# Attention and mixture-of-experts on one core: the first expert's weight matrix in one load, the second batch's keys ahead of it

## Chip, core and metric

The kernel runs on one core of a Trainium2 chip. The metric is the device time of the run in microseconds. Five engines work side by side, each in its own fixed order of instructions: TensorE (PE, matrix products; PEld is its weight load), VectorE (DVE), ScalarE (ACT), GpSimd (POOL) and SyncE (SP). Sixteen DMA engines move data between the main memory (HBM) and the memory on the core; here GpSimd issues all loads and SyncE (at the end also ScalarE) the stores.

## The reference

Eight batches of 576 rows pass through an attention with pooled keys and values (eight heads, width 64), and the result, 4608 rows of 512, goes through a router that picks one of eight experts for each row.

```python
k_p = k.reshape(B, H, Sp, pool, D).mean(axis=3)      # 576 keys -> 72
v_p = v.reshape(B, H, Sp, pool, D).mean(axis=3)
scores = scale * np.matmul(q, k_p.transpose(0, 1, 3, 2))
attn = softmax(scores)                               # written out in the reference
x = np.matmul(attn, v_p)                             # as rows: (B*S, H*D)
...
logits = xn @ en.T / tau                             # cosine of row and expert
expert_idx = np.argmax(logits, axis=1)
h = np.maximum(x[mask] @ w1[e], 0.0)                 # w1[e]: 512 x 1024
out[mask] = gate_w[mask, None] * (h @ w2[e])         # w2[e]: 1024 x 512
```

## The kernel before

Each batch is one unit of work. All of its rows are sent through one guessed expert; the gate of a row whose expert is another one is zero, and a loop at the end adds what other experts owe. That loop isn't entered with these inputs.

**Stages of a batch b.** `attention(b)` loads keys (`load_k`), values (`load_v`) and queries (`load_q`), with a cast from float32 to float16 on the way. DVE adds the keys in groups and turns them (`k0`, `k1`, `kT`: L402 to L423), turns the queries in three units (`q0` to `q2`, L432), and adds the values (L445, L449). The mean of the values gives a guess of the expert (`mean`, `guess`, `guess_out`, L616 to L669). PE computes scores (L478), ACT the exponentials (L487), PE the weighted values (L498); DVE scales them (L508, L510) and turns them into `xt_all` (L533), three units again. Then the routing: squares on ACT (L539), products on PE (L553), and the gate on DVE and GpSimd (L570 to L609). `ffn(b)` makes h = relu(x w1) in eight parts (PE L782, ACT L790/L792), then y = h w2 in five row blocks (PE L801, L830; ACT L818/L839), and stores.

**Weights.** Four pairs of buffers (`held`) keep w1 and w2 of the last four batches' experts. Buffer 0 alone stores w1 in two halves of 512 columns, and `load_w1` fills it with two DMAs; the other three take w1 in one. The parts 0 to 3 of h wait for `lw1`, the parts 4 to 7 for `lw1b`, which is the same step except where b is 0 or 4. From batch 1 on a load is skipped when one of the four buffers already holds that expert; then DVE copies it (`copy_w`, L693) or nothing is to be done.

**Order of the loads.** Every load is a step of GpSimd, and `load()` chains each behind the one before, so their order is the order of the calls at L1036 and after. A step `reg` reads the guessed expert into a register of GpSimd and so holds the queue until the guess is there. Before the change the order at the start is: keys 0, a third of queries 0, values 0, the rest of queries 0, values 1; then `reg` 0, both halves of w1, keys 1, w2, queries 1, values 2; then `reg` 1, the next w1, keys 2, queries 2, w2, values 3.

**Order of all else.** `Plan` holds the steps with estimated durations, priorities and what they depend on. `order` simulates the engines and always takes the step that can start first, with the priority between those that can start at nearly the same time. `improve` then changes priorities at random for 400 rounds, with a fixed seed, and keeps what its model finds no slower. The instructions are emitted in that order; the engines don't reorder. Where the model sees the PE idle, above all in the first 28 us, `warm` (L371) puts dummy products in.

Of the kernel before, what the change touches and what calls it, by code (L numbers as in the profile page):

```python
# [12 lines left out]
FP16 = mybir.dt.float16  # L13
# [229 lines left out]
def kernel(  # L243
# [18 lines left out]
    F = moe_w1.shape[2]  # L262
# [12 lines left out]
    keep = ctx.enter_context(tc.tile_pool(name="keep", bufs=1))  # L275
# [15 lines left out]
    loads = {}  # L291
# [3 lines left out]
    def flat(a, b):  # L295
        return a[b].rearrange("h (i t) d -> (h i) (t d)", t=T)

    def grouped(a, b):
# [3 lines left out]
    NW = 4  # L302
# [1 line left out]
    code_c = keep.tile([1, NW, NW], FP32)  # L304
    weights = {}

    held = [(keep.tile([128, 2, 4, F // 2] if i == 0 else [128, 4, F], FP16, name=f"w1_{i}"),
             keep.tile([128, 4, 2, DM], FP16, name=f"w2_{i}")) for i in range(NW)]

    def w1_view(i):  # L310

        return held[i][0].rearrange("p h k f -> p k h f" if i == 0 else
                                    "p k (h f) -> p k h f", f=F // 2)

    def load_w1(i, e_val, half, cond=None):

        src = moe_w1[ds(e_val, 1)].squeeze(0).rearrange("(p w) f -> p w f", w=4)
        w1 = held[i][0]
        return nc.gpsimd.dma_start(  # L319
            out=w1[:, half] if i == 0 else w1, cond=cond,  # L320
            in_=src[:, :, ts(half, F // 2)] if i == 0 else src)

    def load_w2(w2, e_val, cond=None):
        return nc.gpsimd.dma_start(
            out=w2, cond=cond,
            in_=moe_w2[ds(e_val, 1)].squeeze(0).rearrange(
                "(w p r) d -> p w r d", p=128, r=2))
# [49 lines left out]
    def load(us, dma, emit, after=(), eng='POOL', hit=None):  # L377

        dma_last[0] = plan.step(eng, us, emit, after, dma=dma, seq=dma_last[0],
                                hit=hit)  # L380
        return dma_last[0]


    done = plan.named

    def attention(b, early=False):

        st = {}
# [290 lines left out]

        def weigh(i):  # L680

            w2 = held[b % NW][1]
            ld = (load_w1(b % NW, st['e'], i, st['miss']) if i < 2
                  else load_w2(w2, st['e'], st['miss']))
            st.setdefault('loads', ([], []))[i // 2].append(ld)

        def copy_w():
            code = reg(st['codes'][0:1, 0:1], ENG.DVE, NW)
# [67 lines left out]
    def ffn(plan, b, xt, w, get_gm, finish, last=False, early=0):  # L756
        st = {}
        w1v = w1_view(w).rearrange("p k h (w c r) -> p k h w r c", r=2, c=128)
        w2 = held[w][1]
        pri = 0.0 if b is None else float(b)  # L760

        def before(*names):
            return [] if b is None else [n if isinstance(n, tuple) else (n, b)
                                         for n in names]

        def h_part(w, u):


            if u == 0:
                st['ph', w] = psum(plan)  # L770
            ph = st['ph', w]
            for kk in range(4):
                x = xt()[:, kk]
                if w >= early:
                    to, of = ph[:, ds(u * 512, HALF)], x[:, ts(u, HALF)]
                elif u == 2:
                    to, of = ph[:, 512:256 + S], x[:, 256:S]
                else:
                    ms = (slice(0, 96), slice(96, 128))[u]
                    to, of = (a.rearrange("p (h m) -> p h m", h=2)[:, :, ms]  # L780
                              for a in (ph[:, 256:512], x[:, 0:256]))
                nc.tensor.matmul(out=to, lhsT=w1v[:, kk, w // 4, (w // 2) % 2, w % 2, :],  # L782
                                 rhs=of, start=(kk == 0), stop=(kk == 3))
# [62 lines left out]
        def chain(us, emit, after=(), tiles=0):  # L846
            o = plan.step('PE', us, emit, [*prev[0], *after], pri, tiles)
            prev[0] = [o]
            return o
# [4 lines left out]
        hs, relus = {}, []  # L854
        for w, u in order:
            end = 2 if w < early else 1
            xs = before('lw1' if w < 4 else 'lw1b', 'copy',
                        *(f'x{i}' for i in range(u + 1 if w < early else u + 2)))
            hs[w, u] = chain((0.33, 0.24, 0.54)[u] if w < early else 0.495, lambda w=w, u=u: h_part(w, u), xs,
                             tiles=int(u == 0))  # L860
            if u == end:
                if b is not None:
                    done['h', w, b] = hs[w, u]
                relus.append(plan.step('ACT', 0.57, lambda w=w: relu(w), [hs[w, u]], -10 + pri,
                                       frees=[(hs[w, 0], 0)]))
# [7 lines left out]
        for part in parts:  # L873
# [5 lines left out]
            c, half = part  # L879
# [34 lines left out]
    with tc.manual_schedule():  # L914
        def load_k(b, after=()):
            def emit():
                kk = loads['k', b] = inp.tile([128, T * D], FP16, name="kk")
                nc.gpsimd.dma_start(out=kk, in_=flat(k, b))
            done['lk', b] = load(0.6, 3.05, emit, [('k1', b - 2), *after])
# [22 lines left out]
        def load_expert(b, part=None):  # L942
            st = routes[b]
            if part in (None, 0):
                done['reg', b] = load(2.0 if b else 1.3, 0.0, st['chosen'],
                                      [('ix' if b == 0 else 'eb', b)])
            after = [('reg', b), ('y', b - NW)]
            us = (2.8, 2.8, 5.7) if b % NW == 0 else (5.6, 0.0, 5.7)
            for i, name in enumerate(('lw1', 'lw1b', 'lw2')):
                if us[i] == 0.0:  # L950
                    done[name, b] = done['lw1', b]
                elif part in (None, i // 2):
                    done[name, b] = load(0.65, us[i], lambda i=i: st['weigh'](i), after,
                                         hit=(b, 0.45, 0.02) if b > 1 else None)

        def first(eng, us, emit, after=(), dma=0.0):
# [46 lines left out]
        def pairs():  # L1003
# [11 lines left out]
            out=emb_h, in_=emb, func=AF.Square, accum_out=emb_n), [o_emb])  # L1015
# [4 lines left out]
            out=emb_n, in0=emb_n, in1=half_c[:E, 0:1], op=ALU.pow), [o_sq, o_ones])  # L1020
# [3 lines left out]
            out=ident_h, in0=irow, scalar1=icol, scalar2=None, op0=ALU.is_equal), [o_iota])  # L1024
# [8 lines left out]

        for b in range(B):
            attention(b, early=(b == 0))
        load_expert(0, 0)  # L1036
        load_k(1)
        load_expert(0, 1)
        load_q(1)
        load_v(2)  # L1040
        load_expert(1, 0)
        load_k(2)
        load_q(2)
# [57 lines left out]
    with tc.For_i(0, n_val[0], 1) as i:  # L1101
        f_val = nc.values_load(ext_i[0:1, ds(i, 1)], min_val=0, max_val=1)
        with tc.If(f_val > 0):
            b_val = nc.values_load(pair_b[0:1, ds(i, 1)], min_val=0, max_val=B - 1)
            e_val = nc.values_load(pair_e[0:1, ds(i, 1)], min_val=0, max_val=E - 1)
            for half in range(2):
                load_w1(0, e_val, half)
            load_w2(held[0][1], e_val)
            xt_c = inp.tile([128, T * D], FP16, name="qq").rearrange("p (w s) -> p w s", w=4)
            nc.vector.tensor_copy(  # L1110
                out=xt_c, in_=xt_all[:, ds(b_val, 1)].squeeze(1))
            gmx = rt.tile([128, NC], FP32, name="gm")
            nc.vector.tensor_copy(
                out=gmx,
                in_=oh_all[:, ds(b_val, 1), :, ds(e_val, 1)].rearrange("p b c e -> p (b c e)"))
            nc.vector.tensor_tensor(
                out=gmx, in0=gmx,
                in1=gate_all[:, ds(b_val, 1)].squeeze(1), op=ALU.mult)
            o_b = out[ds(b_val * S, S)]

            def add_rows(c, y_sb):
                o_sb = yp.tile([128, DM], FP32, name="y_sb")
                cols = DM if c < 4 else DM // 2
                for src, dst in out_rows(o_b, c, o_sb):
                    nc.sync.dma_start(out=dst, in_=src)
                nc.vector.tensor_tensor(out=y_sb[:, 0:cols], in0=y_sb[:, 0:cols],
                                        in1=o_sb[:, 0:cols], op=ALU.add)
                for dst, src in out_rows(o_b, c, y_sb):
                    nc.sync.dma_start(out=dst, in_=src)

            def finish(c, y_sb):
                if c != 3:
                    add_rows(c, y_sb)
                    return

                with tc.If(b_val < B - 1):
                    add_rows(c, y_sb)
                with tc.If(b_val > B - 2):
                    nc.vector.tensor_tensor(out=y_end, in0=y_end, in1=y_sb, op=ALU.add)

            px = Plan()
            ffn(px, None, lambda: xt_c, 0, lambda: gmx, finish)
            px.run()

# [37 lines left out]
```

The softmax here doesn't subtract the row's maximum and nothing guards it: scores larger than these inputs give would overflow.

## Time and profile before

The median of three runs is 213.88 us (213.76 to 214.06); the profiled execution has a span of 212.1 us.

| stretch, us | PE busy | DVE busy | ACT busy | granted PE clock | DMA, GB/s |
|---|---|---|---|---|---|
| 0 to 10 | 8.25 | 4.51 | 2.02 | 1.00 | 127 |
| 10 to 20 | 8.53 | 5.43 | 3.06 | 0.66 | 144 |
| 20 to 30 | 6.58 | 8.38 | 2.56 | 0.50 | 209 |
| 30 to 40 | 9.93 | 4.48 | 6.63 | 0.81 | 213 |
| 40 to 50 | 9.68 | 7.76 | 5.03 | 1.00 | 217 |
| 50 to 60 | 8.81 | 8.59 | 7.11 | 1.00 | 246 |

Each row is ten microseconds of the span, the busy columns are microseconds in it. PE's time includes the dummy products: 8.71 us in the first 11 us, 1.64 us from 20 to 30, 2.05 us from 50 to 60, 1.46 us from 100 to 102, none elsewhere. A line of the timeline reads: start, duration, engine, source line, operation, result and inputs, how many, and in brackets how long the engine was idle before and what ended it. L319 is the load of w1, L324 that of w2, L918 of keys, L932 of queries, L925 of values.

### The profile page before, as it was taken

Reading aid. Unit: us, or ns where it says so; the run is one execution under the profiler, and the core shown is the slowest. Engines: PE = TensorE matmul, PEld = TensorE weight load, DVE = VectorE, ACT = ScalarE, POOL = GpSimd, SP = SyncE. Lnnn points to the kernel's source line nnn. Section 1 sums busy time; section 2 is a strip of 40 time slices with the busy share of each in tenths; the row PEclk is TensorE's granted clock in tenths of the full one; section 3 lists DMA queues with packets and bytes.
Section 4 is the critical chain, followed back from the end, with each engine's and each line's share of the span. In section 5 each row is a group of like instructions: output and inputs, shape, how many; then the busy total and the mean of one; then the engine's idle time right before and its main releaser. Section 6 shows DMA issues by size and latency. Waiting matters only on the chain.

```text
span 212.1 us, 7648 instructions
## 1 busy us (share of the span) xinstructions
PE 192.6 (91%) x3270; PEld 119.9 (57%) x3271; DVE 145.8 (69%) x415; ACT 123.9 (58%) x195; POOL 38.9 (18%) x69
## 2 busy tenths in 40 slices
PE   6979849999898899999899899999899999999970
PEld 2455527646476467556575467646664677467520
DVE  2756793669798956975997689879778989106020
ACT  3024226585576568668583597657786689556420
POOL 7308041302220044003203302400200020002000
PEclk9975558999999999999999999999999999999995
DMA  4996999999999149999994899999970510051052
GB/s 77 186 188 104 209 214 207 213 210 247 254 220 162 52 78 204 245 223 252 245 215 43 180 246 255 215 217 246 256 174 3 159 66 6 0 166 61 2 173 57
DMA packets 18182, 34.63 MB, mean 163 GB/s; under 512 B 2008, under 2 KB 9048, under 8 KB 17632
## 3 DMA queue, kind: packets, MB, share of 16 engines
q0 software_dynamic: 12096, 24.65, 62.9%
q1 hardware_dynamic: 5680, 9.00, 13.6%
q8 instruction: 26, 0.43, 0.8%
q10 hardware_dynamic: 368, 0.46, 0.7%
q14 instruction: 12, 0.10, 0.2%
HBM read 61.88 MB, written 9.44 MB: 336 GB/s over the span
## 4 chain that ended last, share of the span: by engine, by line
PE 54%; DVE 7%; ACT 4%; issue 2%; ACTq 0%; DVEq 0%
PE pa L782 21%; PE pa L801 20%; PE pa L498 4%; PE pa L478 3%; PE pa L830 3%; PE pa L553 2%; DVE x_sb L510 2%; DVE vv L445 2%; DVE xt_all L533 1%; ACT at L487 1%; ACT sq L539 1%; DVE rc L508 0%; PE pa L616 0%; ACT y_sb L818 0%; DVE k L414 0%
## 5 line engine op out<-in xcount | busy, mean ns | idle before, releaser
L782 PE MATMUL pa<-xt_all,w 128*128 128x288 f16 (+3 forms) x576 | 71.7, 279 | 4.6 <-DVE xt_all L533 4.5
L782 PEld LDWEIGHTS <-w 128*128 128x128 f16 x576 | 50.2, 100 | 20.3 <-issue 7.1
L801 PE MATMUL pa<-w,hT 128*128 128x512 f16 x256 | 59.5, 380 | 0.4 <-ACT y_sb L818 0.3
L487 ACT ACTIVATE at<-pa 72x768 f16<-72x768 f32 x48 | 36.8, 802 | 10.4 <-PE pa L478 10.3
L792 ACT ACTIVATE hT<-pa 128x576 f16<-128x576 f32 x48 | 31.2, 650 | 13.1 <-PE pa L782 12.7
L801 PEld LDWEIGHTS <-hT 128*128 128x128 f16 x256 | 23.7, 98 | 26.8 <-issue 1.1
L818 ACT ACTIVATE y_sb<-pa,gm 128x512 f32<-128x512 f32 x29 | 19.1, 685 | 25.0 <-PE pa L801 23.6
L533 DVE STREAM_TRANSPOSE xt_all<-x_sb 128x256 f16<-128x256 f16 (+2 forms) x48 | 24.8, 555 | 0.7
L432 DVE STREAM_TRANSPOSE qT<-qq 128x768 f16<-128x768 f16 x24 | 22.5, 958 | 3.0 <-DMA qq<-in_q_dram 2.7
L510 DVE TENSOR_TENSOR x_sb<-pa,rc 128x768 f16<-128x768 f32 x24 | 23.0, 958 | 0.8
L539 ACT ACTIVATE sq<-xt_all 128x1024 bf16<-128x1024 f16 (+1 forms) x16 | 18.6, 1160 | 8.3 <-DVE xt_all L533 8.2
L570 POOL TENSOR_TENSOR rn<-lgT,half_c 128x5 f32<-128x5 f32 x8 | 9.5, 1186 | 62.9 <-DVE lgT L575 62.9
L478 PE MATMUL pa<-qT,kT 32*72 32x192 f16 (+2 forms) x512 | 17.1, 259 | 0.7 <-DVE x_sb L510 0.5
L319 POOL DMA_DIRECT2D w<-in_moe_w_dram x10 | 4.1, 414 | 70.2 <-DMA w<-in_moe_w_dram 23.9
L498 PE MATMUL pa<-vpx,at 72*32 72x65 f16 x1152 | 14.9, 201 | 1.9 <-ACT at L487 1.8
L498 PEld LDWEIGHTS <-at 72*32 72x32 f16 x1152 | 11.8, 100 | 8.2 <-ACT at L487 4.8
L371 PE MATMUL pa<-ones_m 128*128 128x512 f16 x45 | 13.9, 458 | 1.7 <-DVE half_c L1008 1.7
L508 DVE RECIPROCAL rc<-pa 128x12 f32<-128x12 f32 x24 | 5.3, 222 | 14.4 <-PE pa L498 14.0
L478 PEld LDWEIGHTS <-kT 32*72 32x72 f16 x512 | 10.9, 116 | 7.3 <-issue 2.5
L575 DVE STREAM_TRANSPOSE lgT<-pa 128x160 f32<-128x160 f32 x8 | 2.8, 345 | 17.7 <-PE pa L553 17.7
L925 POOL DMA_DIRECT2D vv<-in_v_dram x16 | 10.5, 670 | 16.0 <-DMA w<-in_moe_w_dram 6.7
L445 DVE TENSOR_TENSOR vv<-vv 72x2048 f16<-72x2048 f16 (+1 forms) x14 | 13.1, 938 | 0.3
(99 smaller groups left out, 160.4 us busy)
## 6 DMA issues: line engine op xcount, KB each, us to landing
w<-in_moe_w_dram POOLq DMA_DIRECT2D x14, 1024.0 KB, 15.9
out_dram<-y_sb SPq DMA_DIRECT2D x30, 256.0 KB, 7.3
kk<-in_k_dram POOLq DMA_DIRECT2D x8, 576.0 KB, 15.2
vv<-in_v_dram POOLq DMA_DIRECT2D x8, 512.0 KB, 24.4
qq<-in_q_dram POOLq DMA_DIRECT2D x7, 576.0 KB, 15.7
w<-in_moe_w_dram POOLq DMA_DIRECT2D x4, 512.0 KB, 5.7
out_dram<-y_sb SPq DMA_DIRECT2D x15, 64.0 KB, 8.4
vv<-in_v_dram POOLq DMA_DIRECT2D x8, 64.0 KB, 10.5
```

Source lines behind the costliest of these rows:

```text
L432: nc.vector.transpose(out=qT.rearrange("p w r (t i) -> p t w r i", i=16), in_=qq.rearrange("p t (w r i) -> p t w r i", w=2, r=2))
L445: nc.vector.tensor_tensor(out=vv[:, :, 0:n], in0=vv[:, :, 0:n], in1=vv[:, :, n:2 * n], op=ALU.add)
L478: nc.tensor.matmul(out=pS[a // 2][0:G, ds(a % 2 * 512 + r * SU + c0, n)].rearrange(dst, **dd), lhsT=kT[ts(a, 32), w, r, :], rhs=qT[ts(a, 3 ...
L487: nc.scalar.activation(out=at.rearrange("g a r c -> g a (r c)"), func=AF.Exp, scale=escale, in_=st['pS', u][p][0:G].rearrange("g (a c) -> ...
L498: nc.tensor.matmul(out=px[ts(a, 32), c0:c0 + D + 1], lhsT=st['at', u, a // 2][:, a % 2, r, ts(j, 32)], rhs=st['vpx'][:, 2 * a + r, 0:D + 1 ...
L510: nc.vector.tensor_tensor(out=x_sb, in0=pxv[:, :, :, 0:D], in1=rc.unsqueeze(3).to_broadcast([128, 2, 6, D]), op=ALU.mult)
L533: nc.vector.transpose(out=to, in_=of)
L539: nc.scalar.activation(out=st['sq'][:, :, cs], in_=xt_all[:, b, :, cs], func=AF.Square)
L782: nc.tensor.matmul(out=to, lhsT=w1v[:, kk, w // 4, (w // 2) % 2, w % 2, :], rhs=of, start=(kk == 0), stop=(kk == 3))
L792: nc.scalar.activation(out=hT.rearrange("p (r c) -> p r c", c=HALF), func=AF.Relu, in_=st['ph', w].rearrange("p (r c) -> p r c", c=512)[:, ...
L801: nc.tensor.matmul(out=py, lhsT=st['hT', w // 4][:, (w // 2) % 2, w % 2, ts(c, 128)], rhs=w2[:, w // 2, w % 2, :], start=(w == 0), stop=(w ...
L818: nc.scalar.activation(out=y_sb, in_=py, func=AF.Copy, scale=g)
```

## The change

Buffer 0 gets the same layout as the others, so w1 is one load in all four, and `lw1b` disappears: all parts of h wait for `lw1`. In the first and fifth batches there is one load step fewer. The keys of batch 1 move ahead of the first expert's `reg` and weights, so that they don't have to wait until the guess is known. The planner's estimates are adapted (1.8 for the first `reg`, 5.5 for each weight load).

```diff
-    held = [(keep.tile([128, 2, 4, F // 2] if i == 0 else [128, 4, F], FP16, name=f"w1_{i}"),
+    held = [(keep.tile([128, 4, F], FP16, name=f"w1_{i}"),
...
-    def load_w1(i, e_val, half, cond=None):
-
-        src = moe_w1[ds(e_val, 1)].squeeze(0).rearrange("(p w) f -> p w f", w=4)
-        w1 = held[i][0]
+    def load_w1(i, e_val, cond=None):
         return nc.gpsimd.dma_start(
-            out=w1[:, half] if i == 0 else w1, cond=cond,
-            in_=src[:, :, ts(half, F // 2)] if i == 0 else src)
+            out=held[i][0], cond=cond,
+            in_=moe_w1[ds(e_val, 1)].squeeze(0).rearrange("(p w) f -> p w f", w=4))
...
-            xs = before('lw1' if w < 4 else 'lw1b', 'copy',
+            xs = before('lw1', 'copy',
...
-                done['reg', b] = load(2.0 if b else 1.3, 0.0, st['chosen'],
+                done['reg', b] = load(2.0 if b else 1.8, 0.0, st['chosen'],
                                       [('ix' if b == 0 else 'eb', b)])
             after = [('reg', b), ('y', b - NW)]
-            us = (2.8, 2.8, 5.7) if b % NW == 0 else (5.6, 0.0, 5.7)
-            for i, name in enumerate(('lw1', 'lw1b', 'lw2')):
-                if us[i] == 0.0:
-                    done[name, b] = done['lw1', b]
-                elif part in (None, i // 2):
-                    done[name, b] = load(0.65, us[i], lambda i=i: st['weigh'](i), after,
+            for i, name in enumerate(('lw1', 'lw2')):
+                if part in (None, i):
+                    done[name, b] = load(0.65, 5.5, lambda i=i: st['weigh'](i), after,
                                          hit=(b, 0.45, 0.02) if b > 1 else None)
...
+        load_k(1)
         load_expert(0, 0)
-        load_k(1)
         load_expert(0, 1)
```

More of the change, by code (lines that the diff above doesn't have):

```diff
@@ L305 @@
     weights = {}
-    held = [(keep.tile([128, 2, 4, F // 2] if i == 0 else [128, 4, F], FP16, name=f"w1_{i}"),
+    held = [(keep.tile([128, 4, F], FP16, name=f"w1_{i}"),
              keep.tile([128, 4, 2, DM], FP16, name=f"w2_{i}")) for i in range(NW)]
     def w1_view(i):
-        return held[i][0].rearrange("p h k f -> p k h f" if i == 0 else
-                                    "p k (h f) -> p k h f", f=F // 2)
-    def load_w1(i, e_val, half, cond=None):
-        src = moe_w1[ds(e_val, 1)].squeeze(0).rearrange("(p w) f -> p w f", w=4)
-        w1 = held[i][0]
+        return held[i][0].rearrange("p k (h f) -> p k h f", f=F // 2)
+    def load_w1(i, e_val, cond=None):
         return nc.gpsimd.dma_start(
-            out=w1[:, half] if i == 0 else w1, cond=cond,
-            in_=src[:, :, ts(half, F // 2)] if i == 0 else src)
+            out=held[i][0], cond=cond,
+            in_=moe_w1[ds(e_val, 1)].squeeze(0).rearrange("(p w) f -> p w f", w=4))
     def load_w2(w2, e_val, cond=None):
@@ L680, in weigh @@
         def weigh(i):
[L682 to L685, printed above, removed]
+            ld = (load_w2(held[b % NW][1], st['e'], st['miss']) if i
+                  else load_w1(b % NW, st['e'], st['miss']))
+            st.setdefault('loads', ([], []))[i].append(ld)
         def copy_w():
@@ L1105 @@
             e_val = nc.values_load(pair_e[0:1, ds(i, 1)], min_val=0, max_val=E - 1)
-            for half in range(2):
-                load_w1(0, e_val, half)
+            load_w1(0, e_val)
             load_w2(held[0][1], e_val)
```

## The prediction

> **What bounds the kernel now.** I read the busy shares first, then the 40 slices, because an average hides a start that differs from the rest.
>
> ```profile
> PE 192.6 (91%) x3270; PEld 119.9 (57%) x3271; DVE 145.8 (69%) x415; ACT 123.9 (58%) x195; POOL 38.9 (18%) x69
> PEclk9975558999999999999999999999999999999995
> DMA  4996999999999149999994899999970510051052
> ```
>
> TensorE (PE) is busy for 91% of the span, so the end is set by its work plus the holes in it. The granted clock is half in slices 4 to 6 (about 16 to 32 us). Then the windows of ten microseconds: from 30 to 200 us the PE is idle for 6.1 us in all, and the first three windows hold 1.75, 1.47 and 3.42 us. A part of its busy time is filler, the dummy products of `warm` (L371): 3.5 us of it after 50 us. Next the DMA view of 15 to 32 us, 40 columns of 0.425 us, where the change acts:
>
> ```profile
> DMA  8700000599999999999999999989999999999999
> ```
>
> The rings stand empty from about 15.9 to 18.0 us, a hole of 2.1 us, and are full afterwards. The timeline names what ends the hole:
>
> ```profile
> 7.03 0.23 POOL L1005 IOTA pair_e<- 1x64 int32 x1
> 16.65 1.53 POOL L319 DMA_DIRECT2D w<-in_moe_w_dram  x2 [9.38 <-issue]
> 18.17 0.55 POOL L918 DMA_DIRECT2D kk<-in_k_dram  x1
> ```
>
> GpSimd sits for 9.38 us in `reg` until the first expert is known, and the second batch's keys stand behind it in the queue although they need nothing. Last, the timeline of PE and DVE, to see whether the first expert's weights are what the PE waits for:
>
> ```profile
> 25.55 1.44 PE L782 MATMUL pa<-xt_all,w 128*128 128x192 f16 x8
> 27.16 1.01 DVE L533 STREAM_TRANSPOSE xt_all<-x_sb 128x512 f16<-128x512 f16 x2
> 29.82 0.37 PE L782 MATMUL pa<-xt_all,w 128*128 128x64 f16 x4 [2.83 <-DVE xt_all L533]
> 36.63 0.35 DVE L575 STREAM_TRANSPOSE lgT<-pa 128x160 f32<-128x160 f32 x1 [3.47 <-PE pa L553]
> 40.76 2.69 DVE L432 STREAM_TRANSPOSE qT<-qq 128x768 f16<-128x768 f16 x3
> 56.82 1.74 PE L782 MATMUL pa<-xt_all,w 128*128 128x320 f16 x12 [0.91 <-DVE xt_all L533]
> ```
>
> No. The first eight products start at 25.55 with no wait. Dense work starts at 29.82, after 2.83 us on DVE's last transposes of x. By the semaphore updates of the trace the halves of the first w1 landed at 22.3 and 25.9. The second stall is the one that interests me: in the window of 51 to 58.5 us the PE is idle for 7.5 - 6.31 = 1.2 us and fills 2.05 us, because x of batch 1 isn't ready. Its chain begins with the transposes of q at 40.76.
>
> **What the Trainium skill says.** "DMA: Bandwidth & Descriptors", section "Queues, rings and completion order": on each DMA engine descriptors are consumed in ring order. So the keys, issued first, go ahead of w1 and can delay it. The trace agrees: the last updates come in the order of issue, first w1 22.3 and 25.9, keys 28.0, w2 33.4, q 37.0, v 39.7, next w1 44.4. The same page, section "Bandwidth", has 6.15 us for 1 MB; the trace has about 5 us for a whole w1 here, which I use. "TensorE: Matmul & The Clock Gate", Part 1, says that the full clock returns after about 3.4 us of sustained work. The trace agrees: work is dense from 29.82 and the clock share is 0.50 up to 33, 0.64 in the next microsecond, 1.00 after it. Nothing in the change brings that forward.
>
> **The change, part by part.**
>
> *Keys of batch 1 ahead of `reg`.* GpSimd is free at 7.3, and a second kk buffer is fresh, so they are issued there at 0.55 us, in time that is idle now. They queue behind the values of batch 1, whose landing is at 16.3 to 16.8. A transfer of 576 KB takes 2.75 us, the step between the earliest updates of keys and of the second half of w1 (23.81 to 26.56). They land at about 16.3 + 2.8 = 19 instead of 28.0. The hole is filled.
>
> *First w1 whole.* One issue of 0.6 us replaces two (1.53 us): 0.9 us less on GpSimd, hidden by the full rings. The page's packet times are by size in the trace: 1024 bytes take 98 ns, 8192 bytes 625 ns. Two halves are 64 small packets an engine, 6.3 us of packet time; whole it is 8 large ones, 5.0 us. The observed steps are smaller (about 5.6 for both halves), so I take a saving of 0.6 us, between 0 and 1.3. The start: the keys' data end near 18, the issue at 16.65 lets data flow at about 18.0 as now. So w1 is whole at about 18.0 + 5.0 + 1 = 24.0 to 25.0. The early products, which now need only the half that landed at 22.3, start at 25.55 today: they lose nothing at 25, and up to about 1 us at a late end of 26.5, which the wait until 29.82 absorbs.
>
> *Everything queued behind.* w2, q, v of the start come earlier by keys plus saving, 2.75 + 0.6 = 3.4 us: w2 at 30.0 (used at 39.84, no gain by itself), q at 33.6, v at 36.3. The next w1 waits for the second expert (issue 28.23), yet the rings still hold work then, so that group too comes some 3 us earlier.
>
> *What that is worth.* DVE idles 3.47 us ahead of 36.63, and now q isn't there (37.0). With q at 33.6, its three transposes, 2.69 us, fit into that hole, and with them the scores and exponentials of batch 1 can start up to 6 us earlier. The stall at 51 to 58 is 3.2 us. That is the upper bound of this step.
>
> *What it may cost.* Adding, halving and turning the keys takes 0.71 + 0.46 + 0.78 + 0.77 = 2.7 us of DVE, today at 30.3 to 33.2, where nobody waits for them. With the keys there at 19, the planner will set them between 20 and 30 us, where DVE is busy for 8.38 of 10. 1.6 us fit, 1.1 us don't, and they push the last transposes of x and with them the dense start. A price of 0 to 1.1 us; I take 0.8.
>
> *The order.* `Plan.improve` draws its random changes over the list of steps. Two steps (`lw1b` of batches 0 and 4) vanish and one is moved, so the draws differ and all engines' orders are found anew. Idle time and filler from 30 to 200 us are 6.1 + 3.5 = 9.6 us, what an order can win at the utmost. I take +-1.5 us for a new draw.
>
> *The rest.* For batch 4 one skipped load fewer, 94.29 to 94.80, 0.5 us on an idle GpSimd: nothing. The weight copies (L693, 1.22 us each) and PE's weight reads have the same sizes: nothing. The loop over other experts isn't entered.
>
> Sum of the likeliest case: of the 3.2 us about two thirds is won at 51 to 58 (-2.1), since the later stages are held by DVE, busy 8 to 9 of 10 there, and give some back; dense start +0.8. -1.3 us: 213.9 - 1.3 = 212.6.
>
> **The rivals.**
>
> *Hidden anyway (no change).* The page says that PE waits for no DMA but for v at the start (1.5 us). If the planner keeps the transposes of q behind the gate of batch 0, as at 40.76, earlier landings only lengthen the time that data lie there. Against it: DVE takes what can start first, and q would be there before the routing result. Time: 213.9.
>
> *Slower.* DVE becomes the bound of the start: the key work goes ahead of x, +1.1 us, and the new order moves the stalls elsewhere without winning the one at 51 us. The whole w1 also takes away the slack that early products have with a half. For it: DVE's 8.38 of 10 and its fixed order, in which a step that waits holds up all behind it, as with the second guess now (1.02 us idle ahead of 25.73, with x waiting). Time: 213.9 + 1.1 = 215.0, with an unlucky order up to 216.
>
> *Faster at full.* All of the 3.2 us and no price at the start: 210.7.
>
> **How the numbers follow.** Likeliest -1.3: 40%; full gain 15%; no change 13%; slower 32%. The faster cases give 0.55, within 0.2% (0.43 us) 0.13, slower 0.32. The range goes from 210.6 (full gain) to 215.5 (slower with part of the unlucky order).
>
> **What would show it.** Keys issued near 7 us and no hole in the DMA row at 16 to 18; the first w1 landed by 25 us; the group of w2, q, v some 3 us earlier; q of batch 1 turned ahead of the first routing result (L575); fewer fillers and no wait at 51 to 58. The slower case shows as a dense start of L782 past 30.5, with kk work (L402, L408, L414) between the x steps. I am wrong if dense work starts at the same time, q is turned early, and the PE's idle time later grows all the same: then the order found anew decides, not the loads.

## The result, and the profile after

The changed kernel takes 210.76 us (median of four runs, 210.49 to 211.59) beside 213.97 us for the kernel before: ratio 0.9846, interval 0.9802 to 0.9891. Run once more beside the experiments it gave 210.03 us and a ratio of 0.9868 (0.9811 to 0.9925). So the change makes the kernel about 1.3 to 1.5% faster.

Repeats of one kernel lie in steps here: of 98 runs of the kernel before, those with a mean clock share of 0.948 or more took 211.5 to 212.8 us (one took 213.84), those at 0.941 to 0.945 took 213.1 to 214.3 us, and the 14 at 0.936 or 0.937, which the ratios leave out as slow, 215.0 to 215.8 us. One profile against another is therefore good to about 2 us, and the ratios with their intervals decide.

The page after, the same rows as before:

```profile
PE 192.9 (92%) x3281; PEld 118.9 (57%) x3282; DVE 145.4 (70%) x415; ACT 124.0 (59%) x195; POOL 38.1 (18%) x67
PEclk9985589999999999999999999999999999999996
DMA  4999999899999249999998999999940600061052
```

PE's busy time is the same to 0.3 us while the span went from 212.1 to 208.8. That sum hides two things: the dummies rose from 45 to 56 (13.9 to 17.5 us), and the half clock ends 6.5 us sooner (27.2 in place of 33.7 us; the sixth slice has an 8). The DMA view of 15 to 32 us, 40 columns of 0.425 us:

```profile
DMA  9999999984997999799599999999999999999999
```

The hole of 2.1 us has gone. The timeline shows the first loads of GpSimd, then PE and DVE where the prediction looked:

```profile
7.20 0.59 POOL L913 DMA_DIRECT2D kk<-in_k_dram  x1
16.38 0.54 POOL L315 DMA_DIRECT2D w<-in_moe_w_dram  x1 [8.58 <-issue]
34.43 0.61 POOL L315 DMA_DIRECT2D w<-in_moe_w_dram  x1
...
22.72 7.14 PE L367 MATMUL pa<-ones_m 128*128 128x512 f16 x22
29.92 0.49 PE L777 MATMUL pa<-xt_all,w 128*128 128x192 f16 x4
...
24.84 1.04 DVE L529 STREAM_TRANSPOSE xt_all<-x_sb 128x512 f16<-128x512 f16 x2
31.30 0.17 DVE L641 MAX8 mx<-pa 128x8 f32<-128x8 f32 x1 [3.24 <-PE pa L634]
32.83 0.35 DVE L571 STREAM_TRANSPOSE lgT<-pa 128x160 f32<-128x160 f32 x1
37.95 2.69 DVE L428 STREAM_TRANSPOSE qT<-qq 128x768 f16<-128x768 f16 x3
```

Three readings. The keys go out at 7.20. DVE has all of x of batch 0 turned by 25.9 (24.84 + 1.04), against 30.4 before, and the second guess (MAX8) comes after it, at 31.30 instead of 25.73. And yet h starts at 29.92, because 22 dummies keep the PE from 22.72 on. The queries of batch 1 are still turned after the routing result, at 37.95.

Progress is best read from the first product of each batch's last row block (L830 before, L825 after), where the PE ends a batch's y:

| batch | 0 | 1 | 2 | 3 | 4 | 5 | 6 | 7 |
|---|---|---|---|---|---|---|---|---|
| before, us | 49.90 | 77.03 | 97.39 | 122.22 | 144.48 | 166.52 | 187.21 | 198.98 |
| after, us | 49.71 | 74.12 | 96.50 | 118.31 | 140.51 | 162.91 | 183.63 | 195.40 |
| gained so far | 0.2 | 2.9 | 0.9 | 3.9 | 4.0 | 3.6 | 3.6 | 3.6 |

The gain comes in two places, batch 1 (of which 2 us are given back in batch 2) and batch 3; from batch 4 on both kernels run at the same pace. Batch 3 is a stall that the prediction hadn't looked at. The timeline of the kernel before there:

```profile
97.39 1.06 PE L830 MATMUL pa<-w,hT 128*64 128x256 f16 x16
98.39 0.83 PE L782 MATMUL pa<-xt_all,w 128*128 128x192 f16 x8
99.16 0.74 PE L498 MATMUL pa<-vpx,at 72*32 72x65 f16 x48
99.83 0.41 PE L782 MATMUL pa<-xt_all,w 128*128 128x64 f16 x8
100.08 1.46 PE L371 MATMUL pa<-ones_m 128*128 128x512 f16 x6
102.31 0.97 PE L782 MATMUL pa<-xt_all,w 128*128 128x320 f16 x6 [0.78 <-DVE xt_all L533]
```

The last weighted values of batch 3 (L498) come after y of batch 2 is done; h then waits for DVE to scale and turn them, 2.2 us of dummies and idling (100.08 to 102.31). After the change they come before, and h runs on. The order already differs further ahead: DVE turns the first queries of batch 3 at 81.81 in place of 85.75, and PE has its first scores at 83.05 in place of 87.80.

```profile
94.65 0.56 PE L494 MATMUL pa<-vpx,at 72*32 72x65 f16 x48
95.55 1.02 PE L796 MATMUL pa<-w,hT 128*128 128x512 f16 x4 [0.34 <-ACT y_sb L813]
96.50 1.06 PE L825 MATMUL pa<-w,hT 128*64 128x256 f16 x16
97.50 2.65 PE L777 MATMUL pa<-xt_all,w 128*128 128x192 f16 x28
```

### The profile page after: what moved, and what is told of

Read it like the earlier page. It is cut to its first block, busy times and chain, and to the rows that moved or that the text cites. A ratio compares the mean times of both kernels' runs of the same rounds, so it can differ in the third digit from the quotient of the medians.

```text
span 208.8 us, 7667 instructions
## 1 busy us (share of the span) xinstructions
PE 192.9 (92%) x3281; PEld 118.9 (57%) x3282; DVE 145.4 (70%) x415; ACT 124.0 (59%) x195; POOL 38.1 (18%) x67
## 4 chain that ended last, share of the span: by engine, by line
PE 53%; ACT 5%; DVE 5%; issue 2%; ACTq 0%; DVEq 0%
PE pa L796 21%; PE pa L777 19%; PE pa L474 4%; PE pa L494 3%; PE pa L825 3%; PE pa L549 2%; ACT sq L535 2%; ACT y_sb L813 1%; ACT at L483 1%; DVE qT L428 1%; DVE vv L441 1%; DVE x_sb L506 0%; ACT y_sb L834 0%; DVE k L410 0%; DVE kT L419 0%
## 5 line engine op out<-in xcount | busy, mean ns | idle before, releaser
L777 PE MATMUL pa<-xt_all,w 128*128 128x288 f16 (+3 forms) x576 | 69.5, 273 | 0.8 <-DVE xt_all L529 0.8
L777 PEld LDWEIGHTS <-w 128*128 128x128 f16 x576 | 48.6, 98 | 15.0 <-issue 2.8
L483 ACT ACTIVATE at<-pa 72x768 f16<-72x768 f32 x48 | 36.8, 802 | 9.7 <-PE pa L474 9.5
L787 ACT ACTIVATE hT<-pa 128x576 f16<-128x576 f32 x48 | 31.2, 650 | 13.6 <-PE pa L777 13.5
L428 DVE STREAM_TRANSPOSE qT<-qq 128x768 f16<-128x768 f16 x24 | 22.6, 959 | 3.2 <-DMA qq<-in_q_dram 2.8
L367 PE MATMUL pa<-ones_m 128*128 128x512 f16 x56 | 17.5, 480 | 1.7 <-DVE half_c L1000 1.7
L494 PE MATMUL pa<-vpx,at 72*32 72x65 f16 x1152 | 14.3, 201 | 2.2 <-ACT at L483 2.1
L315 POOL DMA_DIRECT2D w<-in_moe_w_dram x8 | 3.1, 391 | 58.5 <-DMA w<-in_moe_w_dram 19.1
L367 PEld LDWEIGHTS <-ones_m 128*128 128x128 f16 x56 | 6.3, 119 | 10.7 <-issue 6.3
```

Of the source, the lines that this page charges most:

```text
L367: nc.tensor.matmul(out=pa[:, 0:512], lhsT=ones_m[:, 0:128], rhs=ones_m[:, 0:512], start=True, stop=True)
L428: nc.vector.transpose(out=qT.rearrange("p w r (t i) -> p t w r i", i=16), in_=qq.rearrange("p t (w r i) -> p t w r i", w=2, r=2))
L483: nc.scalar.activation(out=at.rearrange("g a r c -> g a (r c)"), func=AF.Exp, scale=escale, in_=st['pS', u][p][0:G].rearrange("g (a c) -> ...
L494: nc.tensor.matmul(out=px[ts(a, 32), c0:c0 + D + 1], lhsT=st['at', u, a // 2][:, a % 2, r, ts(j, 32)], rhs=st['vpx'][:, 2 * a + r, 0:D + 1 ...
L787: nc.scalar.activation(out=hT.rearrange("p (r c) -> p r c", c=HALF), func=AF.Relu, in_=st['ph', w].rearrange("p (r c) -> p r c", c=512)[:, ...
```

## The experiments

Two things changed at once, the loads and, through the planner with its new list of steps and its adapted estimates, the order of every engine. The first theories: **1**, the earlier loads themselves are the gain, as predicted; **2**, the dummies are, by bringing the PE's clock up sooner; **3**, the new order is. "Replanned" means that the planner made a new order for the variant; the others keep an order and alter one thing in it.

**Loads alone, order kept.** The step `lk` of batch 1 moves in the finished order to just ahead of the step `reg` of batch 0:

```diff
-        for o, slots, idle, spare in self.order(bias)[1]:
+        out = self.order(bias)[1]
+        at = {o['i']: n for n, (o, _, _, _) in enumerate(out)}
+        keys, reg = (at[self.named[x]['i']] for x in (('lk', 1), ('reg', 0))) if ('lk', 1) in self.named else (0, 0)
+        if keys > reg:
+            out.insert(reg, out.pop(keys))
+        for o, slots, idle, spare in out:
```

> The kernel before, with one thing altered: the keys of batch 1 are issued ahead of the first reg, after the planner has made its order; both halves of w1 and the order of every other engine stay as they were. Theory 1 (earlier loads are the gain, as the prediction had it): q and v land some 3 us earlier, time falls by 1 us or more, 212.9 or less. Theory 2 (the PE clock is the gain: dummy products ahead of the first expert bring it to full 6.5 us sooner): no gain, 213.7 to 214.1, clock at half until about 33.7 us. Theory 3 (only the new order found by the planner counts): no gain either, 213.7 to 214.1.

213.55 us, ratio 0.9989 (0.9955 to 1.0024): no gain that can be told. The loads did come sooner; by the trace's semaphore updates the keys landed at 20.0 in place of 28.0, w2 at 31.4 in place of 33.4, q at 34.6 in place of 37.0. DVE made no use of it:

```profile
36.78 0.35 DVE L580 STREAM_TRANSPOSE lgT<-pa 128x160 f32<-128x160 f32 x1 [2.97 <-PE pa L558]
40.87 2.69 DVE L437 STREAM_TRANSPOSE qT<-qq 128x768 f16<-128x768 f16 x3
```

It idles for 2.97 us ahead of the routing result with q there from 34.6, since q's transposes stand behind that result in its order. Theory 1 as it stood (a gain of 1 us or more, some 0.5%) is refuted.

**The clock alone.** Dummies in the PE's hole of the kernel before, at the second unit of h of batch 0:

```diff
+            if b == 0 and w == 0 and u == 1:
+                for _ in range(14):
+                    nc.tensor.matmul(out=ph[:, 0:256], lhsT=ones_m[:, 0:128], rhs=ones_m[:, 0:256],
+                                     start=True, stop=True)
```

> The kernel before, with 14 dummy products of 256 columns put into the PE's hole of 2.83 us ahead of the 29.8 us mark (their results are never read); loads and order as before. Theory 2 (clock): full clock at about 27 to 29 us in place of 33.7; the 3.9 us of dense work that ran at half clock takes 1.9 us less: 212.0. Theories 1 (loads) and 3 (order): no gain, 213.9, or 0.2 more where the dummies overrun the hole.

212.81 us, ratio 0.9979 (0.9955 to 1.0003). In the profile the full clock came during the microsecond 26 to 27, in place of 33 to 34, so the clock was moved as meant, but it is worth between nothing and 0.45%, short of the 0.9% that theory 2 gave it and of the change's 1.3 to 1.5%. (In its profile the last row blocks of batches 0 and 7 start at 47.62 and 197.37, 2.3 and 1.6 us ahead of the kernel before. That is more than the ratio shows, and about what two profiles of one kernel can differ by.)

**The dummies taken out of the changed kernel:**

```diff
+        if 18 < t < 30:
+            n = 0
```

> The changed kernel without the 22 dummy products ahead of the first expert's h; loads and order as in the changed kernel. They kept the PE from 22.7 to 29.9 us, while w1 had landed at 25.0 and x of all rows at 25.9. Theory 2 in its plain form (the clock they bring is the gain): the gain of 3.2 us is lost in good part, 212.5 to 213.5. Theory 2 with its price (h starts at 25 in place of 29.9, runs at half clock for some 3.5 us and then at full): 4.9 us sooner, 1.8 us lost to the clock, a net gain on the changed kernel of up to 3 us, 208 to 209.5. Theory 1: the dummies only cost, 206 to 208.

210.69 us, ratio 0.9877 (0.9825 to 0.9929), not told apart from 0.9846 and 0.9868 with them. None of the three expectations fits. What shows is a swap: the PE now starts h 4.3 us sooner, at the landing of w1, and at half clock.

```profile
25.59 0.82 PE L779 MATMUL pa<-xt_all,w 128*128 128x192 f16 x4 [3.57 <-DMA w<-in_moe_w_dram]
```

```profile
PEclk9995559999999999999999999999999999999997
```

Two things are to be seen: w1 whole is now really waited for (3.57 us), where the half had landed in time; and starting sooner at half clock and starting later at full clock come out even as far as the intervals tell. So the 22 dummies aren't the gain, and no loss from them shows.

**Each half of the change, replanned.** Keys early, w1 in halves:

```diff
+        load_k(1)
         load_expert(0, 0)
-        load_k(1)
         load_expert(0, 1)
```

> Half of the change: keys of batch 1 ahead of the first reg, in the planner's list of steps so that a new order is found, with w1 in two halves as before. The planner now sets 13 dummies ahead of h in place of 3. Theory 1 (loads): most of the gain, 211 to 212. Theory 2 (clock): part of it, since 13 dummies at half clock last 5.6 us, full clock at about 27 to 29: 211 to 212.5. Theory 3 (order): anything from 212 to 215.5.

210.11 us, ratio 0.9894 (0.9835 to 0.9953): most or all of the gain, and a time below all three expected ranges. And w1 whole with the keys in their old place (the changed kernel with `load_k(1)` put back behind `load_expert(0, 0)`; the adapted estimates stay):

> The other half of the change: w1 whole in all four buffers, keys of batch 1 still behind the first w1, new order by the planner. It has 22 dummies ahead of h as the changed kernel, and DVE turns all of x of batch 0 ahead of the second guess as there, but keeps the dummies of the later stall in batch 3. Theory A (the early keys let the planner find the better order): no gain, 213.3 to 214.5. Theory B (any new draw, or the DVE order at the start alone): 210.5 to 212.

214.94 us, ratio 1.0100 (1.0056 to 1.0144): slower, by more than either theory had it. The stall of batch 3 is there as in the kernel before, though x of batch 0 is done by 26.2, ahead of the second guess at 30.9:

```profile
98.35 0.56 PE L494 MATMUL pa<-vpx,at 72*32 72x65 f16 x48
98.84 0.41 PE L777 MATMUL pa<-xt_all,w 128*128 128x64 f16 x8
99.09 1.46 PE L367 MATMUL pa<-ones_m 128*128 128x512 f16 x6
101.33 1.74 PE L777 MATMUL pa<-xt_all,w 128*128 128x320 f16 x12 [0.79 <-DVE xt_all L529]
```

So with these draws the keys carry the gain, and w1 whole (with the adapted estimates, which weren't tried apart) costs when it comes alone. Together with the first experiment this means: the keys help only through the order that the planner makes when it knows of them.

**The order without the early landing.** The changed kernel's order, keys issued behind the first w1 when the program is written out:

```diff
+            keys = next(x for x in out if x[0] is self.named['lk', 1])
+            out.remove(keys)
+            at = next(n for n, x in enumerate(out) if x[0] is self.named['lw1', 0])
+            out.insert(at + 1, keys)
```

> The changed kernel with its planned order on every engine, but the keys of batch 1 issued behind the first w1 when the program is written out. Keys land near 27 to 28 us in place of 19 to 20, w1 some 2 us sooner, w2 and q up to 2 us later because of the hole. DVE takes the keys at 26.8 and the PE has dummies until 29.9, so at most 1 us of waiting on DVE. If the order is the gain and not the landing: 210.5 to 211.5. If the early landing itself is needed: 212.5 or more.

211.33 us, ratio 0.9893 (0.9859 to 0.9928). The order brings most of the gain with the keys landing at 27.8. Between this ratio and those of the changed kernel lie 0.25 to 0.5%, which the intervals don't tell apart from nothing; if the early landing adds anything, it is of that size. My working in the expectation was off for w1: it landed at 25.1, not sooner than in the changed kernel.

**One stretch of the order in the kernel before.** The second guess behind the last turn of x on DVE, with the GpSimd steps that hang on it:

```diff
+            a = next(n for n, x in enumerate(out) if x[0] is self.named['eb', 1])
+            z = next(n for n, x in enumerate(out) if x[0] is self.named['x1', 0])
+            late = [x for x in out[a:z] if x[0] is self.named['eb', 1] or x[0]['eng'] == 'POOL']
+            out[a:z + 1] = [x for x in out[a:z + 1] if x not in late] + late
```

> The kernel before, with one stretch of the DVE order altered: the guess of batch 1 (MAX8 to the copy of its index, 1.4 us, with 1.0 us of waiting ahead of it) goes behind the last scaling and turning of x of batch 0, as in the changed kernel. Loads, w1 in halves and all other engines' orders stay. If this is where the gain of the start comes from: x is whole some 2.4 us sooner, 28.0 in place of 30.4, dense work starts by 28 and 1 to 2 us are gained, 212 to 213. If the gain is in the later stalls: 213.5 to 214.

211.69 us, ratio 0.9942 (0.9912 to 0.9972): 0.3 to 0.9% from moving ten small instructions. DVE and PE in the timeline:

```profile
26.91 1.10 DVE L539 STREAM_TRANSPOSE xt_all<-x_sb 128x256 f16<-128x256 f16 x3
27.93 0.14 DVE L651 MAX8 mx<-pa 128x8 f32<-128x8 f32 x1
...
27.40 6.12 PE L788 MATMUL pa<-xt_all,w 128*128 128x64 f16 x36 [0.43 <-DVE xt_all L539]
```

x is whole at 28.0 in place of 30.4, and the PE's wait of 2.83 us has become 0.43. This is a bit under half of the change's gain. (The full clock came at 31.7 in place of 33.7 in this profile; before_filled, which brought it to 26.6, gained 0.45% at the most.) The stall of batch 3 stayed (six dummies from 98.1), and the rest of the difference arises there: at batch 2 this kernel is 0.9 us ahead of the changed one (95.60 against 96.50), at batch 3 it is 1.9 us behind (120.25 against 118.31).

**Is it only a lucky draw?** The planner's search is random, so its seed was altered (`seed=1` to `seed=2`) in each of the four combinations; the unaltered changed kernel ran again beside the last three.

> The kernel before with another seed of the planner's search (2 in place of 1), so other draws and another order; loads as before. Theory B (a new draw of the order is as likely to win or lose): anywhere from 211.5 to 215.5, and a result at 211 or less would show that the change's gain is within what a draw does. Theory A (early keys are needed for the better order): 213 to 215.

> The changed kernel unaltered, so that it stands beside runs of the kernel before on the same chip as the experiments do: 210.3 to 211.3, about 0.985 of the kernel before.

> The changed kernel with seed 2 of the planner's search. Theory A (early keys let the planner find the better order whatever the draws): 210 to 212.5, at least 2 us below the kernel before with the same seed (214.8). Theory B (the gain was a lucky draw): 213 to 215.

> Early keys with w1 in halves, new order with seed 2. Theory A: 210 to 212. Theory B: 213 to 215.

> w1 whole, keys behind it as before, new order with seed 2. Theory A: no gain, 213.5 to 215.5. Theory B: anything from 211 to 215.

| ratio to the kernel before | seed 1 | seed 2 |
|---|---|---|
| neither half of the change | 1 | 1.0034 (1.0004 to 1.0064) |
| w1 whole | 1.0100 (1.0056 to 1.0144) | 1.0113 (1.0056 to 1.0170) |
| keys early | 0.9894 (0.9835 to 0.9953) | 1.0074 (1.0043 to 1.0105) |
| both (the change) | 0.9846, again 0.9868 | 0.9867 (0.9812 to 0.9922) |

The medians of the second seed, over all runs, are 214.75, 215.23, 214.22 and 210.39 us, in the order of the rows. The change wins with both seeds and w1 whole alone loses with both. Early keys alone win with one and lose with the other, so theory A (early keys are enough whatever the draw) failed on keys_seed2; theory B (a lucky draw) failed on after_seed2. The halves don't add up: with seed 2 each alone is slower than the kernel before, and both together are 1.3% faster. Which half carries the gain is not settled by these runs. The trace of keys_seed2 says where it loses. The starts of the last row block of batches 3 to 7:

| us | 3 | 4 | 5 | 6 | 7 |
|---|---|---|---|---|---|
| keys early, seed 1 | 117.74 | 139.61 | 162.91 | 183.32 | 195.09 |
| keys early, seed 2 | 118.81 | 140.73 | 165.24 | 186.52 | 198.29 |

At batch 4 the second seed is still 3.8 us ahead of the kernel before (144.48); it loses 1.2 us on its sister in batch 5 and 0.9 in batch 6, long after the loads of the start. In these two profiles it is still 0.7 us ahead at batch 7 (198.29 against 198.98), which is within what two profiles of one kernel can differ by; the ratio over many runs makes it the slower one. The step from batch 2 to batch 3, by contrast, divides all the runs. Wherever the planner knew the keys to be early (both seeds of keys, both of the change, its repeat, its order with late keys or without the dummies) it took 21.4 to 22.6 us; in all the others, before_x_first and before_filled among them, 24.5 to 24.8 us. These are four orders of the planner on each side; the other profiles repeat one of them. So the absence of the stall of batch 3, some 2 to 3 us, held in every draw tried; what comes after is the draw's, and it took back all of it once.

## Why the prediction was right, and where it wasn't

**Direction and range** held: faster, and 210.76 lies in 210.6 to 215.5, at its lower end. The size was short, 1.3 us against 3.2 in the first comparison, and the cause was another one: the early loads, tried alone, gave no gain that can be told (0.9955 to 1.0024). That the time fell into the range is luck; the gain came from a new order, for which the prediction had no direction.

**Transfers: right.** Keys were to land at 19, did by 20.0; w1 at 24 to 25, was 25.0; w2 at 30.0, was 30.7; q at 33.6, was 33.5; v at 36.3, was 36.1. The Trainium skill says in "DMA: Bandwidth & Descriptors", section "Queues, rings and completion order", that each DMA engine takes its descriptors in ring order; it says so of DMAs that SyncE and ScalarE issue, and adds that they need not complete in that order. For these loads, which GpSimd issues, the trace shows that they did: the last updates came in the order of issue. One exception: the next w1 was to come 3 us sooner and landed at 43.1 against 44.4, since the second guess now comes later and holds its issue until 34.43.

**q into DVE's hole: wrong.** This is the step that failed. I wrote that DVE takes what can start first, so q's transposes would go ahead of the routing result. It is the planner that does so, in its model; DVE then runs the fixed order. The transposes went behind the routing result in every run, and keys_moved_only shows q lying there while DVE idles. In the changed kernel q could not have gone ahead: the routing result came at 32.83, q landed at 33.5. It then lay until 37.95, behind the gate.

**The stall at 51 to 58: mis-sized.** In the window 51 to 58.5 the PE's idling is now 0.8 us (7.5 - 6.71) and the dummies there 1.46 us, 2.3 us in place of 3.2. I had counted 2.1 us of gain there; it is 0.9. And this isn't from the loads either: after_keys_late, with q landing at 36.8, has the same 6.71 and 1.46 us there.

**A price of 0.8 us for key work ahead of x: wrong in sign.** The planner set the first key step at 26.8, behind x. The stretch of 20 to 30 us, which I feared for, got shorter, because the second guess moved out of it. I had named its wait (1.02 us ahead of 25.73, with x waiting) in the rival, as an example of what a fixed order costs, and not asked what removing it would bring: before_x_first puts it at 0.3 to 0.9%.

**The new order, +-1.5 us around nothing: mis-sized and mis-centred.** It carried most of the gain, if not all (after_keys_late); four combinations and two seeds spread over 210.0 to 215.2 us. The conclusion of the line about what would prove me wrong ("then the order found anew decides, not the loads") is what happened. Of its three signs only the first came, dense work at the same time (29.9 us); q wasn't turned early, and the PE's idle time didn't grow.

**The clock: half right.** "Nothing in the change brings that forward" was wrong: w1 whole made the model see 5 us of idling, which `warm` filled with 22 dummies (0.22 us each in the model), and the full clock came at 27 instead of 33.7. before_filled and after_unfilled show that it matters little.

**What stays open.** Why the planner finds the better order in batch 3 only with early keys was not taken apart; moving that one stretch by hand was not tried, so its worth of 2 to 3 us is read from the profiles and not shown by an experiment. The adapted estimates alone in the old kernel were not tried. Nor do two seeds give the spread of draws.

## What to carry to other kernels

When a kernel's order comes from a planner, a change of loads is two changes; try it once with the order kept and once with the old loads in the new order before crediting either. On an engine with a fixed order, ask of every small step that waits what stands behind it: here ten small instructions ahead of x held back the PE's dense work by 2.4 us. A load that landed sooner was worth nothing that could be told here while its consumer kept its place in its engine's order.

## What the runs showed of the hardware

**The clock makes steps in the times of an unaltered kernel.** The three groups of the kernel before have medians of 212.0, 213.7 and 215.3 us, at clock shares of about 0.950, 0.943 and 0.937. The half-clock stretch lasted 20.5 us in its profile (13.2 to 33.7) and 13.7 us in that of the changed kernel (13.6 to 27.2); across the profiles of this case the stretches at half clock that begin and end within the run last 3.4, 6.8, 10.2, 13.7, 17.1 or 20.5 us, multiples of about 3.4 us. The Trainium skill ("TensorE: Matmul & The Clock Gate", Part 1) describes a free-running window of 3413 ns that fits these lengths. An estimate from them: one such window more at half clock costs dense PE work 3.4 / 2 = 1.7 us, about the step between the groups. A gain below 1% therefore needs many repeats, or it is the window's phase that is compared.

**Busy time in the profile does not tell the clock.** In the kernel before, the PE is busy for all of the 6.8 us from 13.3 to 20.1, and the clock share stays at 0.50. So the 3.4 us of sustained work that the prediction counts on, taken as busy time, fit the return of the full clock at 33.7 but not this stretch. In keys_replanned the half clock came back for 6.8 us (49.2 to 56.0) after 3.4 us in which the PE was busy for 1.86; yet with 1.88 us of 3.4, from 148.1 to 151.5, the clock stayed full. What sets it off is not shown. That kernel took 210.11 us all the same.
